# Column maxima of attention scores: subtraction on VectorE, or addition of the negated maxima by accumulating DMAs

## The chip, the cores and the metric

The kernel runs on one core of one Trainium2 chip. Its time is the device time of one execution in microseconds (us), lower is better; of several executions the median is taken. The core has five instruction queues: TensorE (PE; its weight loads are shown apart as PEld), VectorE (DVE), ScalarE (ACT), GpSimd (POOL) and SyncE (SP). All run side by side, each strictly in its own written order, and wait for each other by semaphores. SP computes nothing here: it issues DMAs, as POOL does too. The DMAs of both run on the same 16 DMA engines. Matrix products land in PSUM, everything else lives in SBUF or in HBM.

## What is computed

The reference takes a token matrix x (2048 tokens, width 448) and mixes two blocks by a sigmoid gate:

```
g = sigmoid((x * gate_w).sum(-1))
q, k, v = split heads of x @ wqkv          # 16 heads of width 28
a = softmax(q k^T * 28**-0.5) v @ wo       # full attention, 2048 x 2048 per head
b = (relu(x @ W_gate) * (x @ W_up)) @ W_down   # hidden width 1792
out = g * a + (1 - g) * b
```

All inputs and the output are float32. The softmax needs a maximum for each query row so that the exponent does not overflow.

## The kernel before

Keys stand on the partitions and queries along the free dimension: a *score* is a product of K (128 keys) with Q (512 queries), so the exponentials can go into the next product without a transpose. There are 16 heads; each is handled in two *visits* (one for each half of the 2048 keys), and each visit is one *round* of the main loop: 32 rounds, v = 0 to 31. Even rounds start a head, odd ones end it.

**Two ways to a maximum.** For three of the four blocks of 512 queries, `smax` multiplies Q with K once more (`sm`), takes the maximum along the free dimension on DVE (`mx`, line 171), and `smax_end` (`n` in the order strings) turns these row maxima by a small PE transpose (`mt`) and writes them over ACT (`mr`, `mh`), DVE and two DMAs (`Q<-mh`, line 188) into two extra rows of Q, where the score product subtracts them for nothing. This runs one to two heads ahead, and the first score of a new head has to wait for those two rows. For the fourth block of queries (j = 3, `TQ = 1`) the maximum is taken from the scores themselves: the scores are copied raw from PSUM to SBUF by ACT, `block_max` (line 228) folds them on DVE into `rm`, reading PSUM, `all_max` (`A`, line 234) takes the maximum over the partitions on POOL, `take_max` (`d`, line 239) subtracts `rm` from two quads of 128 x 2048 on DVE, and `take_exp` (`e`, line 246) exponentiates them on ACT. `rescale` (`c`, `f`) corrects the first visit's sums when the second visit found a larger maximum.

**The order of the work** is written out by hand. `FIRST`, `LONG`, `WIDE` and `LATE` are strings of one letter per piece of work, and `ROUNDS` says which string each round follows: round 0 is FIRST, the last three are LATE, four are WIDE and 24 are LONG. `s` is a score (two matmuls of 512 columns and the ACT copy or exp), `m` is an `smax` (two matmuls and a reduce), `x` is one matmul of the hidden layer (`gu`; 11 of them make a half unit, two halves a unit), `P` and `Q` are the two halves of the product with V (`po`), `w` prepares weights of the hidden layer (`split_f`: a high part by ACT, the rest `wg` on POOL, line 112). `score` runs `AHEAD` pieces into the next visit. PSUM gives scores and `sm` products three buffers of two banks in turn (`ps_w`), so each of them waits until the piece three places earlier has been read out. For the raw scores of block 3, that means read by ACT and by DVE.

**The DMA queue of SP** carries all loads in written order. `small_things(2v)` stands at a round's start and `small_things(2v + 1)` behind a certain `s`, the eighth. In an even round the first loads K and Q of the head after next (`load_k`, `load_q`: 8 DMAs of 28 rows of 8 KB), the second issues the row sums' reciprocals to HBM and their broadcast back (`l_d`, `rb`: `row_sums`, `spread`); SP waits in between until the first has landed. In the following odd round the first new `m` of the round reads the K and Q so loaded. The tokens X are replaced after each 14th unit (`gu_mm`), and the hidden layer's products go to HBM (`h_d`) until the attention is done. After round 31 the kernel runs the rest of the hidden layer, the output projection and the mix (`acc`, `wo`).

Of the kernel before, what the change touches and what calls it, by code (L numbers as in the profile page):

```python
# [9 lines left out]
F32 = mybir.dt.float32  # L10
# [9 lines left out]
P = 128  # L20
S = 2048
D = 448
H = 16
# [14 lines left out]

EARLY = (5, 4, 4, 3, 2, 2, 1, 1)

AHEAD = 3

NP = 10

FIRST = "AmxmxsmxmxxlxsxumsmmmxxxsxdxxxsxssmxxmxsmmxdexxsxsewsPQ"

LONG = "ssmnAxxxxsmxsxmxsmxxxmsmxxxsmxxmxsdxsxxxsxsmxxxsmxxmexxsmxxdxxcsxsefwsPQ"

WIDE = "smnmxxxxxxxsxxmxxxxmsxmxxsmxxsAmxsxmxxsxsmxdxsxxsssxxxmxxxcsxmsxxdxxmxxxxexsxewsPfQ"

LATE = "snwsxxAxdxxxsxxsxxxsxxdsxxxxcsxxsxxxsxxxsxxxxsxsxxxxsxxxxxexxxsxxessPfQ"
# [15 lines left out]
def gated_mix_kernel(ctx, tc, x, wq, wo, wgu, wd, out):  # L67
# [138 lines left out]

    stream = [p for v in range(2 * H) for p in visit(v)]
    todo_max, todo_sub, todo_exp, todo_all = [], [], [], []
    RM = {}

    def block_max(v, j, k, p, q):

        n = TQ[v // 2]
        b = j - NB + n
        if (v, b) not in RM:
            if b == 0:
                rm = att.tile([P, max(TQ), TB], F32, name=f"rm_{v}", tag=f"rm{v % 2}", bufs=1)
                for c in range(n):
                    RM[v, c] = rm[:, c]
        r = RM[v, b]  # L220
        if k % (NK // 2):
            parts = [(p[:, c], r) for c in range(2)]
        elif v % 2:
            parts = [(p[:, 0], RM[v - 1, b]), (p[:, 1], r)]
        else:
            parts = [(p[:, 0], q[:, 1])]
        for x, y in parts:
            nc.vector.tensor_tensor(r, x, y, op=OP.max)  # L228
        if k % (NK // 2) == NK // 2 - 2:
            todo_all.append((v, b, [(v, j, i) for i in (k // 4 - 1, k // 4)]))  # L230

    def all_max():
        v, b, quads = todo_all.pop(0)
        nc.gpsimd.partition_all_reduce(RM[v, b], RM[v, b], P, bass_isa.ReduceOp.max)  # L234
        todo_sub.extend((v, b, q) for q in quads)

    def take_max():
        v, b, q = todo_sub.pop(0)
        nc.vector.tensor_tensor(QUAD[q], QUAD[q], RM[v, b].unsqueeze(1).to_broadcast([P, 4, TB]), op=OP.subtract)  # L239
        todo_exp.append(q)  # L240

    def take_exp():
        q = min(todo_exp, key=lambda q: (q[0], q[2], q[1]))
        todo_exp.remove(q)
        q = QUAD[q].rearrange("p c t -> p (c t)")
        nc.scalar.activation(q, q, AF.Exp, scale=SCALE)  # L246

    def score(late=True):

        v, done, q, half, chunks = stream.pop(0)  # L250
        h = v // 2
        if q not in QUAD:
            QUAD[q] = p_slot(next(slots) % NP, f"P_{v}_{q[1]}_{q[2]}")
        ps = ps_w(f"s_{v}_{chunks[0][0]}_{chunks[0][1]}")
        for c, (k, j) in enumerate(chunks):
            nc.tensor.matmul(ps[:, c], K[h % 3][:, k * P:(k + 1) * P], Q[h][:, j * TB:(j + 1) * TB], start=True, stop=True)  # L256
            AT[v, k, j] = QUAD[q][:, 2 * half + c]
        dst = QUAD[q][:, 2 * half:2 * half + 2]
        if done:
            nc.scalar.activation(dst, ps, AF.Exp, scale=SCALE)  # L260
        else:
            nc.scalar.activation(dst, ps, AF.Copy)  # L262
            job = (v, chunks[0][1], chunks[0][0], ps if late else dst, dst)
            if late:
                block_max(*job)
            else:
                todo_max.append(job)

    X = {}

# [17 lines left out]
    with tc.tile_pool(name="qkv", bufs=1) as pa:  # L288
# [132 lines left out]

        warm = pa.tile([P, TB], BF16, name="warm")
        nc.vector.memset(warm, 0.0)
        ps = ps_x("warm_ps")
# [51 lines left out]
        for n, (f, *a) in enumerate(mixed):  # L476
            if n == 0:
                split_w(*w5)
            if n == 6:
                load_k(1)  # L480
                load_q(1)
            if n == 8:
                split_w(*w3)
            if n == 13:

                nc.gpsimd.memset(f32(K[2])[96:128], -1.0)
            if n == len(mixed) - 6:
# [8 lines left out]
            news = [(score, False) for back in EARLY if back == len(mixed) - n]  # L496
# [161 lines left out]
    split_f(0, act_high, pool_low, (0,))  # L658
    fetch_f(1)
    while todo_max:  # L660
        block_max(*todo_max.pop(0))
    for v, (order, nu) in enumerate(ROUNDS):
        todo = list(range(nxt, nxt + nu))
        nxt += nu
# [4 lines left out]
        for o in order:  # L669
            if o == "x" and not passes:  # L670
                continue
            if o == "s":
                ns += 1
                if ns == 8:
                    small_things(2 * v + 1)
                if stream:
                    score()
# [17 lines left out]
            elif o == "w":  # L695
                ready = nxt + (ROUNDS[v + 1][1] if v + 1 < len(ROUNDS) else 2)
                ready = min(ready + ready % 2, 2 * NF)
                while parts < ready:
                    split_f(parts // 2, act_high, pool_low, (parts % 2,))
                    parts += 1  # L700
                    if parts % 2 == 0:
                        fetch_f(parts // 2 + 1)
            elif o == "A":
                all_max()
            elif o == "d":
                take_max()
            elif o == "e":
                take_exp()
            elif o in "cf":
# [1 line left out]
            elif o == "l":  # L711
                sends.pop()()
            elif o == "u":
                split_f(0, act_high, pool_low, (1,))
# [8 lines left out]
        left = [k for k in todo_exp + todo_sub + todo_all if k[0] == v]  # L723
        assert not passes and not left and v not in PO or len(stream) == max(0, 16 * (2 * H - 1 - v) - AHEAD), (v, passes, left, len(stream) + 16 * (v + 1))
    assert not stream and m == len(maxima), (len(stream), m)
    stk.close()

# [181 lines left out]
```

## Time and profile before

| | us |
|---|---|
| median of 3 runs | 1289.12 (1284.76 to 1290.27) |
| the profiled execution | 1281.88, span 1280.1 |
| PE busy | 1241.6 (97%) |
| DVE busy | 962.1 (75%) |
| ACT busy | 776.1 (61%) |
| POOL busy | 191.2 (15%) |
| projections, up to the start of the main loop | 0 to about 136 |
| round 0 | about 136 to 177 |
| rounds 1 to 31 | 177 to 1080 |
| rest | 1080 to 1280 |

A row of the profile names engine, line and operation, then what is written and read (`rm<-s,rm`), its shape, how often it ran (x218), busy time and mean duration in ns, then the engine's idle time before it and who ended that. In the chain of waits, each row is a start, a duration and who held the chain: a stretch of DVE there is a time in which PE waited for DVE or worked on something that did not count. The PE matmuls are pipelined, so a row's duration (0.39 us for one) is longer than the spacing of two starts.

### The profile page before, as it was taken

How to read it: one execution, taken by the hardware profiler on the slowest of the kernel's cores; microseconds unless marked ns; L12 is line 12 of the kernel's file. 1: busy time of each engine (PE TensorE's matmuls, PEld its weight loads, DVE VectorE, ACT ScalarE, POOL GpSimd, SP SyncE). 2: the span in 40 equal slices, each digit the busy share in tenths (PEclk: the TensorE clock that was granted, in tenths of full speed). 3: DMA queues.
4: the chain of work that ended last, by engine and by line, in shares of the span. 5: the costliest groups of instructions: out<-in, count | busy, mean ns of one | idle time of the engine just before them, and what ended most of it. 6: DMA issues, size and time to landing. Idle time of an engine off the chain costs nothing.

```text
span 1280.1 us, 16867 instructions
## 1 busy us (share of the span) xinstructions
PE 1241.6 (97%) x6431; PEld 872.5 (68%) x6431; DVE 962.1 (75%) x1022; ACT 776.1 (61%) x894; POOL 191.2 (15%) x188
## 2 busy tenths in 40 slices
PE   9999699999999999999999999999999999999998
PEld 6888466665656666666666566666666566799998
DVE  6466679898988989998988889898989543563342
ACT  5223377777877677777777677767777784122121
POOL 4222221221221000000000001000000010551020
PEclk9999899999999999999999999999999999999999
DMA  9845275352626543342536243342442325745432
GB/s 323 289 189 222 84 209 117 127 163 72 169 76 201 169 121 84 103 133 64 163 104 186 81 113 103 84 130 93 132 128 76 119 90 195 228 147 159 132 115 80
DMA packets 64269, 178.37 MB, mean 139 GB/s; under 512 B 13730, under 2 KB 20578, under 8 KB 59554
## 3 DMA queue, kind: packets, MB, share of 16 engines
q1 hardware_dynamic: 57452, 151.00, 39.5%
q0 software_dynamic: 6304, 25.82, 5.3%
q8 instruction: 51, 0.84, 0.3%
q10 hardware_dynamic: 432, 0.46, 0.1%
q14 instruction: 30, 0.25, 0.1%
HBM read 118.58 MB, written 58.87 MB: 139 GB/s over the span
## 4 chain that ended last, share of the span: by engine, by line
PE 89%; DVE 4%; ACT 2%; DMA 2%; issue 1%; POOL 1%; SPq 0%; POOLq 0%; ACTq 0%
PE gu L547 19%; PE s L256 19%; PE po L601 18%; PE sm L169 13%; PE acc L808 10%; PE qk L381 5%; DVE rm L228 3%; PE wo L767 3%; PE v L399 3%; ACT P L262 1%; DVE mx L171 1%; DMA wg<-ws_d 1%; DMA or<-o_d 0%; DMA wr<-wq 0%; ACT P L260 0%
## 5 line engine op out<-in xcount | busy, mean ns | idle before, releaser
L171 DVE TENSOR_REDUCE mx<-sm 128x1 f32<-128x1024 f32 x384 | 456.5, 1219 | 60.6 <-PE sm L169 59.5
L547 PE MATMUL gu<-X,wg 128*128 128x512 f32 x1232 | 373.9, 398 | 10.8 <-POOL wg L112 7.2
L260 ACT ACTIVATE P<-s 128x1024 f32<-128x1024 f32 x306 | 306.7, 1025 | 116.8 <-PE s L256 113.1
L256 PE MATMUL s<-Q,K 128*128 128x512 f32 x1024 | 319.5, 403 | 13.6 <-DVE rm L228 11.2
L547 PEld LDWEIGHTS gu<-X,wg 128*128 128x128 f32 x1232 | 231.6, 189 | 69.1 <-POOL wg L112 7.6
L256 PEld LDWEIGHTS s<-Q,K 128*128 128x128 f32 x1024 | 184.7, 189 | 99.3 <-DVE rm L228 10.9
L169 PE MATMUL sm<-K,Q 128*128 128x512 f32 x768 | 243.2, 398 | 7.5 <-DVE mx L171 3.6
L601 PE MATMUL po<-P,V 128*32 128x512 f32 x1640 | 227.3, 594 | 0.0
L228 DVE TENSOR_TENSOR rm<-s,rm 128x512 f32<-128x512 f32 x218 | 150.4, 690 | 74.6 <-ACT P L262 57.3
L169 PEld LDWEIGHTS sm<-K,Q 128*128 128x128 f32 x768 | 137.1, 188 | 52.6 <-ACT P L260 10.1
L234 POOL PARTITION_ALL_REDUCE rm<-rm x32 | 57.2, 1788 | 673.7 <-DVE rm L228 618.8
L601 PEld LDWEIGHTS po<-P,V 128*32 128x32 f32 x1640 | 62.6, 110 | 116.2 <-issue 111.5
L808 PE MATMUL acc<-WD,hh 128*128 128x448 f32 x672 | 138.5, 365 | 0.0
L262 ACT ACTIVATE P<-s 128x1024 f32<-128x1024 f32 x104 | 105.1, 1024 | 46.6 <-PE s L256 45.4
L808 PEld LDWEIGHTS acc<-WD,hh 128*128 128x128 f32 x672 | 126.2, 188 | 10.4
L239 DVE TENSOR_TENSOR P<-P,rm 128x2048 f32<-128x2048 f32 x52 | 117.9, 2272 | 5.8 <-POOL rm L234 5.8
L601 PE MATMUL po<-V 128*32 128x512 f32 x408 | 115.0, 594 | 0.0
L103 ACT ACTIVATE hh<-hr 128x512 fp32r<-128x512 f32 x56 | 35.2, 631 | 117.8 <-PE acc L808 113.8
L246 ACT ACTIVATE P<-P 128x2048 f32<-128x2048 f32 x52 | 99.4, 1914 | 5.3 <-DVE P L239 4.5
L260 ACT ACTIVATE V<-s 128x1024 f32<-128x1024 f32 x78 | 78.9, 1025 | 37.1 <-PE s L256 35.2
L109 DVE TENSOR_TENSOR hh<-hr,hh 128x512 fp32r<-128x512 f32 x56 | 49.4, 883 | 62.2 <-ACT hh L103 62.2
L381 PE MATMUL qk<-X,W 128*128 128x512 f32 x308 | 77.4, 398 | 0.3 <-DVE X L109 0.2
(79 smaller groups left out, 772.4 us busy)
## 6 DMA issues: line engine op xcount, KB each, us to landing
wg<-ws_d SPq DMA_DIRECT2D x42, 896.0 KB
K<-qk_d SPq DMA_DIRECT2D x64, 224.0 KB
Q<-qk_d SPq DMA_DIRECT2D x64, 224.0 KB
h_d<-h SPq DMA_DIRECT2D x56, 256.0 KB
hr<-h_d SPq DMA_DIRECT2D x56, 256.0 KB
ws_d<-wg SPq DMA_DIRECT2D x14, 896.0 KB
qk_d<-st POOLq DMA_DIRECT2D x21, 512.0 KB, 3.2
wgr<-wgu SPq DMA_DIRECT2D x13, 512.0 KB
```

What stands on the lines that cost most here:

```text
L169: nc.tensor.matmul(ps[:, c, :], Q[h][:, u * P:(u + 1) * P], K[h % 3][:, k0:k0 + TB], start=True, stop=True)
L171: nc.vector.tensor_reduce(MX[h][:, 2 * u + half:2 * u + half + 1], ps, axis=AX.XY, op=OP.max)
L228: nc.vector.tensor_tensor(r, x, y, op=OP.max)
L239: nc.vector.tensor_tensor(QUAD[q], QUAD[q], RM[v, b].unsqueeze(1).to_broadcast([P, 4, TB]), op=OP.subtract)
L246: nc.scalar.activation(q, q, AF.Exp, scale=SCALE)
L256: nc.tensor.matmul(ps[:, c], K[h % 3][:, k * P:(k + 1) * P], Q[h][:, j * TB:(j + 1) * TB], start=True, stop=True)
L260: nc.scalar.activation(dst, ps, AF.Exp, scale=SCALE)
L262: nc.scalar.activation(dst, ps, AF.Copy)
L381: nc.tensor.matmul(ps, W[:, a, c * P:(c + 1) * P], xf(tb, b), start=(n == 0), stop=(n == NT - 1))
L547: nc.tensor.matmul(ps, WS[i][:, s, a], xf(i // NF, b), start=(n == 0), stop=(n == NT - 1))
L601: nc.tensor.matmul(po[32 * j:32 * j + 32], V[:, h // 4 % 2, k, h % 4], AT.pop((v, k, j)), start=(k == k0), stop=(k == k0 + NK // 2 - 1))
L808: nc.tensor.matmul(ACC[i // NF][t][:, :D], HH[i][:, a, t * P:(t + 1) * P], WD[:, f, b], start=(f == 0 and n == 0), stop=(f == NF - 1 and n ...
```

## The change

Seven things change together:

- **Maxima.** Scores of block 3 are copied with scale -1, so SBUF holds negated raw scores. `block_min` (`b`, three letters per visit) folds them on DVE from SBUF only: three operations of 128 x 1024, one of 128 x 512, and one that negates (and in odd visits takes the maximum with the first visit's). `rm` is the positive maximum as before.
- **Subtraction.** `take_max` now adds `rm` to the negated scores. With letter `d` this is a DMA from POOL that accumulates into SBUF (two of 1 MB per visit); with `g`, in round 0 alone, a DVE operation. The exponent's scale is negated.
- **POOL.** The hidden layer's weight rests (`low`) go from POOL to DVE, and a small all-reduce (`warm_r`) is run at the start of the program.
- **K and Q loads** go from the start of an even round to behind `row_sums` and `spread`, which now stand behind the tenth `s`.
- **Order strings.** All four are rewritten; `AHEAD` is 4, and `n` moves in LONG from the round's start to behind its ninth `s`.
- **WIDE rounds** are k = 2, 7, 10, 19, so that units 13, 27 and 41 end in a round's last `x`: the tokens are replaced there.
- **The extra Q buffer's** constant rows are copied by two DMAs, not set by POOL.

POOL in rounds 1 to 3 before. A bare `ISA` stands where POOL is configured for another kind of instruction; `rm` is the all-reduce, `wg` a weight rest:

```order
L234 ISA
L234 ISA rm_1_1302<-rm_1_1302 128x512
L112 ISA
L112 TENSOR_TENSOR wg_3_1567<-wgr_3_1326,wg_3_1567 128x384 x2
L112 TENSOR_TENSOR wg_3_1567<-wgr_3_1326,wg_3_1567 64x2x128
L234 ISA
L234 ISA rm_2_1553<-rm_2_1553 128x512
```

POOL in the same rounds now (P and V hold the quads):

```order
L238 ISA rm_1_0_1310<-rm_1_0_1310 128x512
L245 DMA P_1_3_2_1266<-rm_1_0_1310 128x4x512
L245 DMA P_1_3_3_1282<-rm_1_0_1310 128x4x512
L238 ISA rm_2_0_1553<-rm_2_0_1553 128x512
L245 DMA V_101<-rm_2_0_1553 128x4x512
L245 DMA P_2_3_1_1534<-rm_2_0_1553 128x4x512
```

The weight rests and the reconfigurations have gone from POOL, and each all-reduce is followed by its two accumulating DMAs.

SP in round 12 before (an even round; `ls` are the sums that the round before made):

```order
L611 DMA ls_5_4095<-os_5_3863 128x1x16
L148 DMA K2_104<-qk_d_71 28x2048 x4
L153 DMA Q2_1200<-Q2_1200 2x2048
L155 DMA Q2_1200<-qk_d_71 28x2048 x4
L566 DMA h_d_18_4174<-h_18_4172 128x512
L539 DMA wg_20_4176<-ws_d_6_2086 128x1792
L617 DMA l_d_5_85<-rq_5_4196 128x16
L623 DMA rb_5_4199<-l_d_5_85 32x512 x4
```

SP in round 12 now:

```order
L618 DMA ls_5_4104<-os_5_3855 128x1x16
L624 DMA l_d_5_85<-rq_5_4194 128x16
L630 DMA rb_5_4197<-l_d_5_85 32x512 x4
L148 DMA K2_104<-qk_d_71 28x2048 x4
L153 DMA Q2_1187<-Q2_1187 2x2048
L155 DMA Q2_1187<-qk_d_71 28x2048 x4
L573 DMA h_d_19_4245<-h_19_4243 128x512
L546 DMA wg_21_4247<-ws_d_7_2109 128x1792
```

The loads of K and Q have moved behind the wait of `rb` for `l_d`, and ahead of the round's last weight load.

PE at the start of round 13 before (a LONG round; `mt_7` is the transpose of head 7's row maxima, `s_14` are scores of that head):

```order
L256 MATMUL s_13_14_3_4340<-Q0_105,K0_102 128x512 x2
L256 MATMUL s_13_8_0_4346<-Q0_105,K0_102 128x512 x2
L169 MATMUL sm_192_4351<-K2_104,Q2_1200 128x512 x2
L181 MATMUL mt_7_4355<-ident_149,m_7_4264 16x128
L547 MATMUL gu_20_0_4365<-X0_111,wg_20_4176 128x512 x2
```

PE in round 13 now, from `mt_7` to the first score of head 7:

```order
L181 MATMUL mt_7_4436<-ident_151,m_7_4295 16x128
L554 MATMUL gu_21_0_4418<-X0_111,wg_21_4247 128x512
L264 MATMUL s_13_14_0_4447<-Q0_105,K0_102 128x512 x2
L169 MATMUL sm_198_4451<-K2_104,Q2_1187 128x512 x2
L554 MATMUL gu_21_0_4418<-X1_112,wg_21_4247 128x512
L264 MATMUL s_13_15_0_4456<-Q0_105,K0_102 128x512 x2
L554 MATMUL gu_21_0_4418<-X0_111,wg_21_4247 128x512 x2
L264 MATMUL s_13_14_2_4462<-Q0_105,K0_102 128x512 x2
L169 MATMUL sm_199_4466<-K2_104,Q2_1187 128x512 x2
L264 MATMUL s_14_0_3_4471<-Q1_106,K1_103 128x512 x2
```

Before, `s_14_0_3` stood 50 rows behind `mt_7`; now 14 matmuls stand between them.

The diff, cut to its core; of the order strings, one is shown:

```
-AHEAD = 3
+AHEAD = 4
-LONG = "ssmnAxxxxsmxsxmxsmxxxmsmxxxsmxxmxsdxsxxxsxsmxxxsmxxmexxsmxxdxxcsxsefwsPQ"
+LONG = "AssdmxxsxxmxscxdxsmsxxxmssxxxmsxmxnxsmxsxxsmsxxxsmsxbbxxsxebxxmfxxmxmxexwPQ"
-ROUNDS = [(FIRST, 2)] + [(WIDE, 4) if k % 7 == 2 else (LONG, 3) for k in range(2 * H - 4)] + [(LATE, 4)] * 3
+ROUNDS = [(FIRST, 2)] + [(WIDE, 4) if k in (2, 7, 10, 19) else (LONG, 3) for k in range(2 * H - 4)] + [(LATE, 4)] * 3
...
+    def block_min():
+
+        if not todo_max:
+            return
+        v, j, p = todo_max[0]
+        b = j - NB + TQ[v // 2]
+        if (v, b) not in R2:
+            R2[v, b] = att.tile([P, 2, TB], F32, name=f"r2_{v}_{b}", tag="r2", bufs=1)
+            left[v, b] = NK // 4 - 2
+            nc.vector.tensor_tensor(R2[v, b], todo_max.pop(0)[2], todo_max.pop(0)[2], op=OP.min)
+            return
+        nc.vector.tensor_tensor(R2[v, b], R2[v, b], todo_max.pop(0)[2], op=OP.min)
+        left[v, b] -= 1
+        if left[v, b]:
+            return
...
+        nc.vector.tensor_tensor(r, r2[:, 0], r2[:, 1], op=OP.min)
+        if v % 2:
+            nc.vector.scalar_tensor_tensor(r, r, -1.0, RM[v - 1, b], op0=OP.mult, op1=OP.max)
         else:
+            nc.vector.tensor_scalar(r, r, -1.0, None, op0=OP.mult)
...
-    def take_max():
+    def take_max(way):
         v, b, q = todo_sub.pop(0)
-        nc.vector.tensor_tensor(QUAD[q], QUAD[q], RM[v, b].unsqueeze(1).to_broadcast([P, 4, TB]), op=OP.subtract)
+        m = RM[v, b].unsqueeze(1).to_broadcast([P, 4, TB])
+        if way == "d":
+            nc.gpsimd.dma_start(QUAD[q], m, accum_op=OP.add)
+        else:
+            nc.vector.tensor_tensor(QUAD[q], QUAD[q], m, op=OP.add)
...
-            nc.scalar.activation(dst, ps, AF.Copy)
-            job = (v, chunks[0][1], chunks[0][0], ps if late else dst, dst)
...
+            nc.scalar.activation(dst, ps, AF.Copy, scale=-1.0)
+            todo_max.append((v, chunks[0][1], dst))
...
+        nc.gpsimd.partition_all_reduce(warm_r, warm_r, P, bass_isa.ReduceOp.max)
...
-        if q == 0 and h and h + 2 < H:
-            load_k(h + 2)
-            load_q(h + 2)
...
         if h and q == 1:
             row_sums(h - 1)
             spread(h - 1)
+            if h + 2 < H:
+                load_k(h + 2)
+                load_q(h + 2)
...
-                if ns == 8:
+                if ns == 10:
                     small_things(2 * v + 1)
...
-                    split_f(parts // 2, act_high, pool_low, (parts % 2,))
+                    split_f(parts // 2, act_high, low, (parts % 2,))
...
-                nc.gpsimd.memset(f32(QS[2])[96:128], 0.0)
+                for a, b in ((GD, 12), (GD + 12, 4)):
+                    nc.sync.dma_start(f32(QS[2])[a:a + b].rearrange("p j t -> p (j t)"), Q[1][GD + 2:GD + 2 + b].bitcast(F32))
```

More of the change, by code (lines that the diff above doesn't have):

```diff
@@ L208, in gated_mix_kernel @@
     todo_max, todo_sub, todo_exp, todo_all = [], [], [], []
[L209 to L224, printed above, removed]
-        else:
[L226 to L230, printed above, removed]
+    RM, R2, left = {}, {}, {}
+    def block_min():
[12 more added lines that the diff above has]
+            return
+        r, r2 = att.tile([P, TB], F32, name=f"rm_{v}_{b}", tag=f"rm{v % 2}{b}", bufs=1), R2[v, b]
+        RM[v, b] = r
+        nc.vector.tensor_tensor(r, r2[:, 0], r2[:, 1], op=OP.min)
+        if v % 2:
+            nc.vector.scalar_tensor_tensor(r, r, -1.0, RM[v - 1, b], op0=OP.mult, op1=OP.max)
+        else:
+            nc.vector.tensor_scalar(r, r, -1.0, None, op0=OP.mult)
+        q = NK // 8 * (v % 2)
+        todo_all.append((v, b, [(v, j, q), (v, j, q + 1)]))
     def all_max():
@@ L245, in take_exp, with score @@
         q = QUAD[q].rearrange("p c t -> p (c t)")
-        nc.scalar.activation(q, q, AF.Exp, scale=SCALE)
-    def score(late=True):
+        nc.scalar.activation(q, q, AF.Exp, scale=-SCALE)
+    def score():
         v, done, q, half, chunks = stream.pop(0)
@@ L423, in gated_mix_kernel @@
         nc.vector.memset(warm, 0.0)
+        warm_r = pa.tile([P, 16], F32, name="warm_r")
+        nc.vector.memset(warm_r, 0.0)
         ps = ps_x("warm_ps")
@@ L495, in gated_mix_kernel @@
                 m += 1
-            news = [(score, False) for back in EARLY if back == len(mixed) - n]
+            news = [(score,) for back in EARLY if back == len(mixed) - n]
             for k, c in enumerate(news):
@@ L722, in gated_mix_kernel @@
                 pv(v, "PQ".index(o))
-        left = [k for k in todo_exp + todo_sub + todo_all if k[0] == v]
-        assert not passes and not left and v not in PO or len(stream) == max(0, 16 * (2 * H - 1 - v) - AHEAD), (v, passes, left, len(stream) + 16 * (v + 1))
+        rest = [k for k in todo_exp + todo_sub + todo_all if k[0] == v]
+        assert not passes and not rest and v not in PO or len(stream) == max(0, 16 * (2 * H - 1 - v) - AHEAD), (v, passes, rest, len(stream) + 16 * (v + 1))
     assert not stream and m == len(maxima), (len(stream), m)
```

22 lines of the change are left out of this document (9 added, 13 removed).

## The prediction

> **What bounds the kernel now.** I read the engines' busy times first, then the chain that ended last, by engine:
>
> ```profile
> PE 1241.6 (97%) x6431; PEld 872.5 (68%) x6431; DVE 962.1 (75%) x1022; ACT 776.1 (61%) x894; POOL 191.2 (15%) x188
> PE 89%; DVE 4%; ACT 2%; DMA 2%; issue 1%; POOL 1%; SPq 0%; POOLq 0%; ACTq 0%
> ```
>
> PE is busy nearly always and holds 89% of the chain, so taking work off DVE is worth nothing by itself. Only the time in which PE is held up can be won. The stretches of round 0 (with the few microseconds ahead of it), of an odd LONG round (15) and of two even ones (16 and 20) show where that is; the columns are the stretch, its length, and the busy time of PE, PEld, DVE, ACT and POOL, then PE's clock, the DMA engines' share and GB/s:
>
> ```profile
> 136.00:177.50 41.50, 29.57 (x134) 17.49 (x133) 28.46 (x32) 19.93 (x27) 10.31 (x11) 0.84 0.43 116
> 588.80:617.70 28.90, 28.21 (x158) 18.34 (x155) 25.44 (x25) 22.02 (x24) 1.78 (x1) 1.00 0.17 58
> 617.70:646.70 29.00, 28.20 (x157) 18.21 (x153) 26.54 (x28) 19.97 (x19) 1.83 (x2) 1.00 0.67 184
> 735.70:764.50 28.80, 28.46 (x157) 18.24 (x153) 25.95 (x27) 20.40 (x20) 1.83 (x2) 1.00 0.46 122
> ```
>
> Round 0 leaves PE idle for 12 of 41.5 us, with its clock down to 0.84. In the others DVE is busy 25.4 to 26.5 of 29 us, close to full itself. The chain of waits through round 15 shows what that costs:
>
> ```profile
> 589.55 1.03 ACT P L262
> ...
> 590.61 0.70 DVE rm L228
> ...
> 591.34 0.70 DVE rm L228
> ...
> 592.17 0.70 PE s L256 x2
> ...
> 597.99 0.70 PE gu L547 x3
> ...
> 610.77 7.00 PE po L601 x64
> 617.77 0.43 PE s L256
> ```
>
> Three `gu` matmuls take 0.70 us, so 0.233 each. A LONG round has 16 `s` and 12 `m` of two matmuls and 33 `x`: 89 x 0.233 = 20.7 us, and 7.0 us of `po`: 27.7 us, against 28.9. So 1.2 us a round are lost, and nearly all of it at the start: `s` waits until ACT has copied the raw score and DVE has folded it twice from PSUM (`rm`). That is the ceiling of a round.
>
> **Round 0: -14 us.** The chain there, then POOL's rows:
>
> ```profile
> 135.68 0.70 DVE rm L228
> ...
> 141.43 1.15 DVE mx L171
> 142.61 1.07 PE sm L169 x2
> ...
> 149.45 6.58 issue
> 156.04 0.98 POOL wg L112
> 157.10 0.73 POOL wg L112
> 157.87 0.79 PE gu L547
> ```
>
> ```profile
> 144.31 1.80 POOL L234 PARTITION_ALL_REDUCE rm<-rm  x1 [5.62 <-DVE mx L171]
> 147.12 0.90 POOL L388 DMA_DIRECT2D qk_d<-pair  x1 [1.01 <-DVE pair L109]
> 156.04 1.78 POOL L112 TENSOR_TENSOR wg<-pair,wg 128x384 fp32r<-128x384 f32 x2 [8.01 <-issue]
> ...
> 186.88 1.80 POOL L234 PARTITION_ALL_REDUCE rm<-rm  x1 [6.83 <-DMA Q<-mh]
> ```
>
> Two things hold PE: a block of `rm` operations (135.7 to 141.4), and a weight rest that POOL starts 8.0 us after it was reconfigured from the all-reduce. The order shows that each such change of kind has a bare `ISA` row on POOL; now there is one at the start and one after round 31. The rest goes to DVE (row below: 0.50 us for 128 x 336), and the folds are spread over six `b`. Floor of the round by the same count: 24 pairs x 0.467 + 22 x 0.233 + 7.0 = 23.3 us, against 41.5. I leave 4 us for what stays in line (all-reduce 1.8 us and a DVE addition, 2.3 us as the subtraction's row below, ahead of the first exp): 27.3 us, so -14. Ends: -10, if the additions hold ACT and PE once more, and -17. The early `warm_r` puts its reconfiguration ahead of POOL's memsets and the first stores of `qk`; five staging buffers at 11 matmuls each cover some 13 us of that. I take 0; if the cover is short, up to +3.
>
> **Folding and subtracting: -17 us.** The groups of instructions (busy us, mean ns of one, idle time before):
>
> ```profile
> L171 DVE TENSOR_REDUCE mx<-sm 128x1 f32<-128x1024 f32 x384 | 456.5, 1219 | 60.6 <-PE sm L169 59.5
> ...
> L228 DVE TENSOR_TENSOR rm<-s,rm 128x512 f32<-128x512 f32 x218 | 150.4, 690 | 74.6 <-ACT P L262 57.3 <-ACT V L262 10.0 <-DVE rm L228 0.5
> ...
> L239 DVE TENSOR_TENSOR P<-P,rm 128x2048 f32<-128x2048 f32 x52 | 117.9, 2272 | 5.8 <-POOL rm L234 5.8
> ...
> L246 ACT ACTIVATE P<-P 128x2048 f32<-128x2048 f32 x52 | 99.4, 1914 | 5.3 <-DVE P L239 4.5
> ...
> L109 DVE TENSOR_TENSOR X<-xr,X 128x1024 fp32r<-128x1024 f32 x6 | 7.3, 1224 | 3.6 <-ACT X L103 3.5
> ...
> L109 DVE TENSOR_TENSOR W<-wr,W 128x336 fp32r<-128x336 f32 x6 | 2.8, 504 | 2.0 <-ACT W L103 1.9
> ```
>
> Per visit the folds were about 7 x 0.69 = 4.8 us and become 3 x 1.22 + 2 x 0.69 = 5.0 us: no gain in DVE's work. The gain is that they read SBUF, so a score's PSUM buffer is free after the 1.03 us copy. The two subtractions, 4.5 us a visit, leave DVE, which falls from some 26 to some 22 us a round; the weight rests add about 0.55 us each in rounds 0 to 8, inside that room. So the two `rm` waits at a round's start go. What is late next is ACT: 16 copies of 1.03 us and two exps of 1.9 us are in the way of the same PSUM buffers, and DVE now does its folds in a bunch ahead of the last `m`. I take half of the 1.2 us ceiling in each of 28 LONG and WIDE rounds: -17. Ends: 0 and -34.
>
> **The accumulating DMAs: 0.** Two of 1 MB a visit, 62 in all. No row shows one; the nearest is a plain 1 MB store from POOL, and the load that SP's queue puts on the DMA engines:
>
> ```profile
> x_d<-X POOLq DMA_DIRECT2D x6, 1024.0 KB, 5.1
> q1 hardware_dynamic: 57452, 151.00, 39.5%
> ```
>
> 5.1 us each from issue to landing, 10.2 us a pair, is the lower end; the upper is open. From the 16th score of a round to the first exp in the next there are 10.7 + 17.7 = 28.4 us of PE's written work (letters times the durations above); copy, fold, all-reduce and issue take 0.6 + 1.0 + 2.6 + 1.8 + 0.9 = 6.9 us of it. So the first quad has 21.5 us and both have 24 us. At 10.2 us they are hidden with room for twice that, and at 24 us a pair every further microsecond is paid in each round. I take the lower end's side, since engines loaded to 39.5% + 62 x 5.1 / 1280 = 64% still have room. The Trainium skill, in "Collectives: The Full Stack", section "The bandwidth ceiling: the fold count and why AG ≠ RS ≠ AR", has it that an add in the DMA path needs two source reads and runs at half a copy's rate; by that the pair would take 20.4 us, still inside the 24, but with the engines at 89%.
>
> **K and Q loads: +2 us.** Round 20 and the start of 21 before:
>
> ```profile
> 737.24 2.37 SPq L148 DMA_DIRECT2D K<-qk_d  x4
> ...
> 749.02 0.35 SPq L617 DMA_DIRECT2D l_d<-rq  x1
> 750.48 1.69 SPq L623 DMA_DIRECT2D rb<-l_d  x4
> ...
> 767.74 1.95 SPq L188 DMA_DIRECT2D Q<-mh  x2
> ```
>
> ```profile
> 746.00:747.00 1.00, 1.00 (x6) 0.79 (x6) 0.83 (x2) 0.98 (x1) 0.00 (x0) 1.00 0.96 205
> 747.00:748.00 1.00, 1.00 (x6) 0.82 (x5) 1.00 (x2) 0.05 (x1) 0.00 (x0) 1.00 0.38 82
> ```
>
> The loads keep the DMA engines full from 738 to 747.5, 10.3 us after the first issue. Now the first K load is issued behind `rb`: `l_d` at 12.1 us into the round (13.3 here; the reciprocal now stands behind the sixth reduce, not the eighth), 1.5 us to land, 1.7 us for `rb`: 15.3 us. Done at 25.6. The first `m` of the new head stands 0.9 us into the next round, at about 28.9. Room: 3.3 us, which the next visit's accumulating DMAs, issued from about 24 us on, eat into. Queued behind the wait on SP are the round's last `h_d` and weight load, needed a unit later. I take 2 us over 13 loads; ends 0 and +13 (1 us each).
>
> **Row maxima of the next head: +6 us.** Before, `mt` at 766.03, and the chain behind it:
>
> ```profile
> 766.03 0.27 PE L181 MATMUL mt<-ident,m 128*16 128x128 f32 x1
> 768.82 0.30 DVE L109 TENSOR_TENSOR mh<-mr,mh 16x128 fp32r<-16x128 f32 x1
> ```
>
> The second `Q<-mh` leaves SP at 769.69, and a small DMA lands in 1.5 us less its issue of 0.35: 4.8 us after `mt`. Then a score 50 rows later waited for it; now 14 matmuls lie between, 14 x 0.233 + 0.27 = 3.5 us. So PE would wait up to 1.3 us in each of the 12 odd LONG rounds, +15. But 1.2 us of the 4.8 are DVE finishing two `rm` and a reduce first, which are gone; I take +0.5 us each. Lower end 0.
>
> **The rest.** Token reloads at a round's end: `gu` waits for them in no row above 1 us, 0. AHEAD, Q's constant rows: 0, covered by PE's own work.
>
> **Sum.** -14 - 17 + 2 + 6 = -23. The profiled execution took 1281.88 us, which gives 1259; the median of the runs shown is 7.2 us above it, and against that the forecast is 1289 - 23 = 1266 us.
>
> **Rivals.**
> - *Slower: the accumulating DMAs crowd out the exps.* They share 16 engines with K, Q, weights and `h_d`. The point from which it decides is a pair taking 24 us from issue to landing. At 27 us, three microseconds in 28 rounds are +84: 1289 - 23 + 84 = 1350. For it: K and Q loads alone keep the engines at up to 0.96 for 10 us of every second round. Against it: over the whole of odd round 15 they stand at 0.17. The Trainium skill's "DMA: Bandwidth & Descriptors", section "Issuing engines are not separate DMA queues", says that POOL's and SP's DMAs run on the same engines and interleave, which would delay both.
> - *About the same: the waits are only exchanged.* Row maxima +15, K and Q loads +13, the rest as forecast: 1289 - 31 + 28 = 1286. For it: room of 3.3 us and a shortage of 1.3 us are both small against what I cannot see.
> - *The whole ceiling:* -17 in round 0 and -34 in the rounds, no new wait: 1238. For it: PE waits for nothing else in these rounds.
> - *It does not do what it says:* PE waits on ACT's copies alone, and only round 0 is won: 1289 - 14 = 1275; inside the forecast's own range.
>
> **Chances.** Forecast 0.50, with a range of its own from 1250 to 1279; ceiling 0.12; exchanged waits 0.16; slower 0.22. From no change, 0.5% is 6.4 us, about what can be told apart here. Exchanged waits lie, with their own spread, mostly within that and in part on the faster side: faster 0.50 + 0.12 + 0.06 = 0.68, same 0.10, slower 0.22. The range runs from 1244 (half of the ceiling) to 1300 (the exchanged waits and the mild end of slower); some 0.05 lie below and 0.15 above.
>
> **What would show it.** Round 0 at 26 to 29 us with PE's clock at 1.00; LONG rounds at 28.2 to 28.6 us; no wait of PE `s` for DVE `rm`; DVE near 840 us busy (962 - 62 x 2.27 + 28 x 0.55 + 32 x 0.2); accumulating DMAs landing within 5 to 11 us; POOL with no idle of 6 to 8 us behind a change of kind before the tail. Wrong would be: ACT waiting for a DMA ahead of the exp, PE `sm` waiting for K or Q at the start of odd rounds by more than 0.2 us, PE `s` waiting for `Q<-mh` by more than 1 us.

## Result and profile after

The changed kernel takes 1353.35 us (median, 1352.82 to 1354.58) against 1287.33 us of the kernel before beside it: ratio 1.051, 95% interval 1.0485 to 1.0541. It is 5% slower; the forecast was 1266 us, in a range of 1244 to 1300. (The scores are what is negated: the DMAs add the maxima as they are.)

The page of the changed kernel, in the order of the prediction's fences: busy times, the chain by engine and by line, the two DMA queues with data, and the accumulating DMAs (count, KB each, median us from issue to landing):

```profile
PE 1259.5 (93%) x6431; PEld 881.2 (65%) x6431; DVE 851.4 (63%) x923; ACT 773.3 (57%) x894; POOL 232.0 (17%) x208
PE 68%; DMA 21%; DVE 4%; SPq 2%; ACT 2%; issue 1%; POOL 0%; DVEq 0%; POOLq 0%
...
q1 hardware_dynamic: 57484, 151.13, 36.8%
q0 software_dynamic: 39040, 90.84, 32.3%
...
P<-rm POOLq DMA_DIRECT2D x50, 1024.0 KB, 12.7
V<-rm POOLq DMA_DIRECT2D x12, 1024.0 KB, 13.8
```

DVE is down by 111 us, about as forecast, and PE is held up all the same: its share falls from 97% to 93%, and DMAs, 2% of the chain before, are 21% now. POOL's queue (q0) has gone from 5.3% to 32.3% of the DMA engines' time. Its line before:

```profile
q0 software_dynamic: 6304, 25.82, 5.3%
```

The waits of PE in the changed kernel, and one of DVE (us in all, how often, longest):

```profile
PE s L264 <- DMA Q<-mh: 41.3, 13, 8.6
PE sm L169 <- DVE mx L171: 15.1, 8, 5.2
PE gu L554 <- DMA X<-x_d: 11.3, 6, 4.7
...
DVE rq L623 <- DMA ls<-os: 27.7, 9, 9.5
```

None of these waits is for the accumulating DMAs. Their consumer, the exp, does not wait at all (the last number is ACT's idle time before it):

```profile
L254 ACT ACTIVATE P<-P 128x2048 f32<-128x2048 f32 x52 | 98.4, 1912 | 0.3
```

Three stretches show the gain and the loss side by side: round 0, the even LONG round 10, and the odd LONG round 15 (stretch, length, busy time of PE, PEld, DVE, ACT and POOL, PE's clock, DMA share, GB/s):

```profile
137.00:168.60 31.60, 24.68 (x133) 13.95 (x132) 30.21 (x32) 20.32 (x27) 4.51 (x5) 1.00 0.55 150
485.43:513.39 27.96, 27.96 (x161) 17.96 (x153) 22.18 (x23) 19.53 (x19) 4.36 (x3) 1.00 0.87 191
633.25:667.66 34.41, 30.71 (x161) 19.94 (x154) 22.09 (x22) 21.98 (x23) 4.58 (x5) 0.90 0.56 137
```

Round 10 has no idle PE left: 27.96 us against 28.9 before, the whole ceiling of 1.2 us within 0.3 us. Round 15 holds the same matmuls and takes 6.45 us more.

**How round 15 loses them.** SP's queue (issues), then the chain of waits, then PE's row of that score (in brackets the idle time before it and who ended it):

```profile
643.51 0.38 SPq L546 DMA_DIRECT2D wg<-ws_d  x1
645.31 1.18 SPq L188 DMA_DIRECT2D Q<-mh  x2
```

```profile
645.95 5.50 DMA Q<-mh
...
651.59 1.19 PE s L264 x2
```

```profile
651.59 1.19 PE L264 MATMUL s<-Q,K 128*128 128x512 f32 x2 [3.70 <-DMA Q<-mh]
```

SP issues a weight load of 896 KB and, 1.8 us behind it, the two small DMAs that carry the row maxima of the next head. These take 5.5 us to land, and the first score of that head waits 3.7 us. The wait costs more than itself, as the clock shows (third number from the end):

```profile
640.00:647.40 7.40, 7.40 (x34) 5.77 (x33) 6.40 (x7) 6.40 (x9) 0.00 (x0) 1.00 1.10 234
647.40:651.60 4.20, 0.50 (x4) 0.09 (x2) 1.22 (x1) 1.08 (x2) 0.00 (x0) 0.82 0.44 176
651.60:656.00 4.40, 4.40 (x11) 3.43 (x12) 0.19 (x1) 2.64 (x3) 0.00 (x0) 0.50 0.00 0
656.00:660.00 4.00, 4.00 (x17) 3.23 (x16) 3.79 (x4) 3.00 (x3) 0.00 (x0) 0.88 0.02 4
```

The DMA engines are full before the wait (in the DMA share, the last number but one, more than 1 means that the packets' times add up to more than the stretch). Counted by queue in the trace, 0.95 of that 1.10 are POOL's queue, the accumulating DMAs: the pair issued at 630.7 moves its packets from 633.2 to 648.5, and half of the weight load's packets of 7 KB, issued at 643.5, start only after 648.0. So `Q<-mh` stands behind a load that the accumulating DMAs hold up. The clock is at 0.50 from 650.2 to 656.9 and at 1.00 again from 657 (0.88 is the mean of a stretch that holds both). PE works 5.3 us of this at half speed, which costs 2.7 us; with the 3.7 us of the wait that is 6.4 of the 6.45 us lost.

**How even rounds lose.** Round 6, SP's issues (the first and the last of four transfers for the hidden layer's weights, `ws_d` and `wgr` in turn, and the row sums) and the chain:

```profile
343.79 0.54 SPq L539 DMA_DIRECT2D ws_d<-wg  x1
...
347.17 1.30 SPq L289 DMA_DIRECT2D wgr<-wgu  x1
348.57 1.17 SPq L618 DMA_DIRECT2D ls<-os  x1
```

```profile
348.57 12.62 DMA ls<-os
...
361.21 0.25 DVE rq L623
361.47 1.09 DVE mx L171
...
362.60 1.22 PE sm L169 x2
```

The row sums `ls`, 8 KB, are queued behind these four, of 512 or 896 KB each, and land after 12.6 us. The accumulating pair issued at 339.6 has its packets on the engines from 341.5 to 358.5, beside them. DVE's reciprocal `rq` waits for them, every later reduce waits behind `rq`, and PE waits 5.2 us for a PSUM buffer that such a reduce still has to read.

### The profile page after: what moved, and what is told of

Same layout as the page of the kernel before. It is cut to its first block, busy times and chain, and to the rows that moved or that the text cites. A ratio compares the mean times of both kernels' runs of the same rounds, so it can differ in the third digit from the quotient of the medians.

```text
span 1351.0 us, 16885 instructions
## 1 busy us (share of the span) xinstructions
PE 1259.5 (93%) x6431; PEld 881.2 (65%) x6431; DVE 851.4 (63%) x923; ACT 773.3 (57%) x894; POOL 232.0 (17%) x208
## 3 DMA queue, kind: packets, MB, share of 16 engines
q1 hardware_dynamic: 57484, 151.13, 36.8%
q0 software_dynamic: 39040, 90.84, 32.3%
## 4 chain that ended last, share of the span: by engine, by line
PE 68%; DMA 21%; DVE 4%; SPq 2%; ACT 2%; issue 1%; POOL 0%; DVEq 0%; POOLq 0%
PE gu L554 14%; PE po L608 14%; PE s L264 12%; PE acc L816 10%; PE sm L169 9%; DMA ls<-os 7%; PE qk L385 5%; DMA Q<-mh 5%; PE wo L775 3%; PE v L403 2%; DMA X<-x_d 2%; DVE mx L171 2%; DMA wgr<-wgu 2%; DMA wg<-ws_d 1%; DMA Q<-qk_d 1%
## 5 line engine op out<-in xcount | busy, mean ns | idle before, releaser
L171 DVE TENSOR_REDUCE mx<-sm 128x1 f32<-128x1024 f32 x384 | 463.1, 1221 | 225.4 <-PE sm L169 222.8
L554 PE MATMUL gu<-X,wg 128*128 128x512 f32 x1232 | 384.5, 406 | 17.4 <-DMA X<-x_d 11.3
L264 PE MATMUL s<-Q,K 128*128 128x512 f32 x1024 | 328.5, 412 | 47.2 <-DMA Q<-mh 41.3
L268 ACT ACTIVATE P<-s 128x1024 f32<-128x1024 f32 x306 | 301.7, 1028 | 115.9 <-PE s L264 109.3
L554 PEld LDWEIGHTS gu<-X,wg 128*128 128x128 f32 x1232 | 237.8, 193 | 81.3 <-DMA X<-x_d 10.8
L264 PEld LDWEIGHTS s<-Q,K 128*128 128x128 f32 x1024 | 188.3, 194 | 132.2 <-issue 54.4
L169 PE MATMUL sm<-K,Q 128*128 128x512 f32 x768 | 245.6, 403 | 20.4 <-DVE mx L171 15.1
L169 PEld LDWEIGHTS sm<-K,Q 128*128 128x128 f32 x768 | 140.1, 192 | 67.0 <-DVE mx L171 19.8
L270 ACT ACTIVATE P<-s 128x1024 f32<-128x1024 f32 x104 | 104.5, 1034 | 61.0 <-PE s L264 58.1
L567 DVE TENSOR_TENSOR h<-gu,rl 128x512 f32<-128x512 f32 x56 | 38.5, 688 | 71.4 <-ACT rl L564 24.0
L385 PE MATMUL qk<-X,W 128*128 128x512 f32 x308 | 77.9, 398 | 0.4 <-DVE X L109 0.2
L245 POOL DMA_DIRECT2D P<-rm x50 | 68.8, 1579 | 8.6 <-POOL rm L238 8.6
## 6 DMA issues: line engine op xcount, KB each, us to landing
P<-rm POOLq DMA_DIRECT2D x50, 1024.0 KB, 12.7
V<-rm POOLq DMA_DIRECT2D x12, 1024.0 KB, 13.8
```

The lines of the kernel that those rows point to most:

```text
L169: nc.tensor.matmul(ps[:, c, :], Q[h][:, u * P:(u + 1) * P], K[h % 3][:, k0:k0 + TB], start=True, stop=True)
L171: nc.vector.tensor_reduce(MX[h][:, 2 * u + half:2 * u + half + 1], ps, axis=AX.XY, op=OP.max)
L245: nc.gpsimd.dma_start(QUAD[q], m, accum_op=OP.add)
L270: nc.scalar.activation(dst, ps, AF.Copy, scale=-1.0)
L385: nc.tensor.matmul(ps, W[:, a, c * P:(c + 1) * P], xf(tb, b), start=(n == 0), stop=(n == NT - 1))
L554: nc.tensor.matmul(ps, WS[i][:, s, a], xf(i // NF, b), start=(n == 0), stop=(n == NT - 1))
```

## Experiments

Two theories stood at first. A: the row maxima are too late by their place in the order, and each wait lowers the clock behind it. B: the accumulating DMAs crowd the 16 DMA engines, and everything that is loaded comes late. Each ratio below is to the kernel before on the same chip, with its 95% interval.

### The row maxima earlier

```
-LONG = "AssdmxxsxxmxscxdxsmsxxxmssxxxmsxmxnxsmxsxxsmsxxxsmsxbbxxsxebxxmfxxmxmxexwPQ"
+LONG = "AssdmnxxsxxmxscxdxsmsxxxmssxxxmsxmxxsmxsxxsmsxxxsmsxbbxxsxebxxmfxxmxmxexwPQ"
```

> The changed kernel, with the letter n of LONG (the transpose of the next head's row maxima) moved from 14 matmuls ahead of the head's first score back to the start of the round. Theory A (scores wait for the row maxima, whose small DMAs are queued behind a weight load, and the clock falls behind each such wait; in the changed kernel these waits are 41 us, and the idle of PE lowers its clock): the wait of scores for Q<-mh falls from 41 us to under 2 us, the odd LONG rounds 5, 7, 13, 17 and 19 from 31.6-36.0 us to 28-30 us, the whole to 1285-1305 us. Theory B (the accumulating DMAs crowd the 16 DMA engines, so that everything which is loaded comes late): the waits move to other loads, and the time stays at 1335 us or above.

Measured: 1329.25 us, 1.033 (1.031 to 1.036). The same round 15, and round 9:

```profile
627.98:656.02 28.04, 28.04 (x161) 18.10 (x154) 22.19 (x22) 21.26 (x23) 4.60 (x5) 1.00 0.63 153
441.66:483.61 41.95, 32.52 (x161) 19.37 (x154) 21.41 (x21) 22.17 (x24) 4.51 (x4) 0.88 0.70 194
```

Round 15 is cured, and so are 13 and 19 (28.0 us each); the whole falls by 24 us only. Round 9 is lost to another load: PE waits there four times, 8.4 us in all, for the tokens X that are replaced at the end of round 8. The wait for `Q<-mh` stays at 23.8 us, in rounds 1, 3, 5, 7, 23, 25, 27 and 29. A explains a third of the 66 us and no more.

### The addition on DVE in all rounds

```
-                take_max(o)
+                take_max("g")
```

> The changed kernel, with all additions of the maxima made by DVE and no accumulating DMA. Theory A: the waits for Q<-mh stay at 20 us or more, since the row maxima are still late; the waits for the row sums ls<-os and for the tokens X shrink; DVE rises to about 960 us; 1310-1340 us. Theory B: the waits for DMAs go altogether, 1260-1285 us.

Measured: 1342.11 us, 1.043 (1.041 to 1.045). Neither theory has it. PE's waits:

```profile
PE s L264 <- DVE mx L171: 33.9, 34, 2.8
PE po L608 <- ACT P L254: 10.1, 5, 2.8
PE s L264 <- DMA Q<-mh: 4.8, 4, 2.1
```

The waits for DMAs are nearly gone, `Q<-mh` too, though `n` stands where it stood: this points to the accumulating DMAs as what made the row maxima late, though rounds that are slower for another reason give the row maxima more time too. The order is laid out for DMAs: an addition of 2.3 us on DVE now stands between reduces that PE needs, and in WIDE and LATE rounds the second one stands so near the round's end that `po` waits for the exp behind it. This run says which waits go with the DMAs, not what they cost.

### The row maxima's DMAs in ACT's queue

```
-            nc.sync.dma_start(f32(Q[h])[GD + r:GD + r + 1], f32(mh)[:, r])
+            nc.scalar.dma_start(f32(Q[h])[GD + r:GD + r + 1], f32(mh)[:, r])
```

> The changed kernel, with the two small DMAs of each set of row maxima issued from ACT's queue in place of SP's; all else, the place of n too, as it is. Theory A, in the form that the two small DMAs wait behind the weight load in the same queue: they land within 3.5 us of the transpose in all rounds, the wait for them falls from 41 us to under 8 us, 1290-1315 us. Theory B (the 16 engines themselves are crowded, whatever the queue): they land as late as before, 1340 us or above.

Measured: 1345.1 us, 1.046 (1.044 to 1.048).

```profile
PE s L264 <- DMA Q<-mh: 14.9, 7, 3.8
...
PE s L264 <- ACT P L268: 9.9, 10, 1.8
```

Away from the weight load the wait falls by 26 us, so a large part of it was the place in SP's queue; the time is as theory B had it all the same. The wait of scores for ACT's copies is new (9.9 us, 0.4 in the changed kernel); that it comes from ACT issuing the two DMAs in its own order is likely but not shown. And the waits that are left still bring the clock down: round 15 takes 33.9 us with two of 0.6 and 1.9 us. Only 8 us are won.

### The WIDE rounds where they were

```
-ROUNDS = [(FIRST, 2)] + [(WIDE, 4) if k in (2, 7, 10, 19) else (LONG, 3) for k in range(2 * H - 4)] + [(LATE, 4)] * 3
+ROUNDS = [(FIRST, 2)] + [(WIDE, 4) if k % 7 == 2 else (LONG, 3) for k in range(2 * H - 4)] + [(LATE, 4)] * 3
```

> The changed kernel, with the WIDE rounds where they stood before (k = 2, 9, 16, 23), so that tokens are replaced in the middle of a round. Theory A: the 22 us for which gu waits for X in rounds 9 and 27 shrink or move, the waits for Q<-mh stay; 1330-1350 us. Theory B: the same within 1335-1355 us, since the accumulating DMAs then meet the token loads elsewhere.

Measured: 1350.33 us, 1.052 (1.049 to 1.055). The wait for X falls from 11.3 to 8.0 us (the 22 us of the expectation count PE's weight loads beside its matmuls), and the ratio is no lower than the changed kernel's 1.051: where tokens are replaced matters little.

So the theories were put anew. C: the accumulating DMAs load the engines so much that SP's loads, and what is queued behind them, come late. D: the places of `n` and of the K and Q loads do it, whatever else runs.

### No addition at all

```
-        if way == "d":
-            nc.gpsimd.dma_start(QUAD[q], m, accum_op=OP.add)
-        else:
+        if way == "g":
             nc.vector.tensor_tensor(QUAD[q], QUAD[q], m, op=OP.add)
```

> The changed kernel with the addition of the maxima left out in rounds 1 to 31 (neither DMA nor DVE does it; the exponentials of block 3 are taken of the raw scores there, so this part of the output is not the reference's). Theory C (the accumulating DMAs load the DMA engines so much that SP's loads, and the small transfers queued behind them, come late): the waits for Q<-mh, ls<-os and X, 41, 28 and 22 us now, fall under 10 us together, LONG rounds 27.9-28.6 us, the whole 1245-1275 us. Theory D (the places of n and of the K and Q loads make the row maxima and the loads late, whatever else runs): Q<-mh still holds scores for 15 us or more, 1295 us or above.

This kernel leaves the addition out in rounds 1 to 31, so its output is wrong there. Measured: 1264.82 us, 0.984 (0.982 to 0.986). Two of PE's waits, and the busy times:

```profile
PE s L262 <- DMA Q<-mh: 6.4, 6, 2.3
...
PE gu L552 <- DMA X<-x_d: 1.1, 1, 1.1
...
PE 1234.4 (98%) x6431; PEld 865.6 (69%) x6431; DVE 849.4 (67%) x923; ACT 769.4 (61%) x894; POOL 150.3 (12%) x146
```

This decides it for C; `rq` too waits for `ls` once, 1.9 us, not nine times. The rest of the change is worth about 20 us, and the accumulating DMAs cost 1353.35 - 1264.82 = 88.5 us (about 86 if the 2.7 us by which the kernel before beside the two differs are taken off). By stretches of the trace (a round ends with its last `po` matmul), in us:

| | before | after | no addition |
|---|---|---|---|
| up to the end of round 0 | 177.0 | 168.6 | 168.7 |
| rounds 1 to 9 | 263.8 | 316.9 | 261.1 |
| rounds 10 to 28 | 557.8 | 578.3 | 547.4 |
| rounds 29 to 31 | 74.5 | 77.9 | 74.5 |
| the rest | 207.0 | 209.4 | 210.0 |

Most of the cost, 56 us, lies in rounds 1 to 9, where SP also carries the weights that are split for the hidden layer (`ws_d`, `wgr`). PE's waits of the two runs differ by 65 us (`Q<-mh` 34.9, reduces 15.1, X 10.2, and 5 us of small ones). The remaining 24 us are the clock, 0.974 against 0.997 over the span: for the same 6431 matmuls PE is busy 25 us longer with the accumulating DMAs (1259.5 against 1234.4 us).

### Plain DMAs in their place

```
-            nc.gpsimd.dma_start(QUAD[q], m, accum_op=OP.add)
+            nc.gpsimd.dma_start(QUAD[q], m)
```

> The changed kernel with plain DMAs in place of the accumulating ones: as many, as large, from the same queue at the same places, but they overwrite the scores with the maxima (this part of the output is not the reference's). Theory C, with the addition as what costs: packets of 2 KB take 84-98 ns against 176-190 ns, the DMAs land in 6-9 us against 12.7, and the waits shrink by half or more: 1275-1315 us. If the number and the bytes alone did it, the time stays at 1340 us or above. Theory D: 1300-1330 us, with the waits for Q<-mh at 20 us or more.

These DMAs overwrite the scores, so this output is wrong too. Measured: 1281.63 us, 0.998 (0.996 to 0.999). The queue with data and the DMAs of this run:

```profile
q0 software_dynamic: 23168, 90.84, 18.6%
...
P<-rm POOLq DMA_DIRECT2D x50, 1024.0 KB, 7.6
```

As many bytes cost 17 us instead of 88. Without them the queue took 5.4% of 1261.6 us, so a plain DMA of 1 MB costs (0.186 x 1278.5 - 0.054 x 1261.6) / 62 = 2.7 us of all 16 engines, and an accumulating one (0.323 x 1351.0 - 68.1) / 62 = 5.9 us. It goes in (39040 - 6304) / 62 = 528 packets, the plain one in 272: nearly all are of 2 KB in the first and of 4 KB in the second, and in the traces they take 184 and about 172 ns on average, so a byte costs about twice as much.

### K and Q loads back at the round's start

```
+        if q == 0 and h and h + 2 < H:
+            load_k(h + 2)
+            load_q(h + 2)
...
-            if h + 2 < H:
-                load_k(h + 2)
-                load_q(h + 2)
```

> The changed kernel with the loads of K and Q back at the start of even rounds, ahead of the row sums. Theory C: they then meet the second half of the previous visit's accumulating DMAs, the row sums come later, the time stays within 1340-1375 us. Theory D: 1325 us or below, since the row sums' chain and the maxima no longer have those loads around them late in the round.

Measured: 1404.23 us, 1.093 (1.091 to 1.096), worse than either theory expected.

```profile
PE sm L169 <- DVE mx L171: 47.1, 15, 7.4
...
DVE os L634 <- DMA rb<-l_d: 63.4, 8, 11.0
...
DVE rq L623 <- DMA ls<-os: 44.5, 14, 9.5
```

With the additions by DMA, 1.75 MB ahead of the row sums delays DVE in 14 rounds, not 9. The move of these loads is a gain of about 51 us under this load.

### One addition by DMA, the other on DVE

On top of the first experiment:

```
-        for o in order:
+        for i_o, o in enumerate(order):
...
-                take_max(o)
+                take_max("g" if order[:i_o].count("d") else o)
```

> The changed kernel with n of LONG back at the round's start (1329 us by itself), and only the first of each visit's two additions as an accumulating DMA, the second on DVE. Theory C: the DMA load of the additions halves, the waits for DMAs fall from 38 us to under 15 us, DVE rises to about 910 us: 1285-1310 us. Theory D: no change to speak of against 1329 us, 1318-1335 us.

Measured: 1325.3 us, 1.030 (1.028 to 1.033). The wait for `Q<-mh` is gone and X is at 5.0 us, but scores wait 28.2 us for reduces and `po` 14 us for the exp: the second addition stands in the wrong place for DVE, as before. So the places were chosen next: DVE is idle for 2.2 us during `po`, right before a round's first `m`. WIDE and LATE got their `A` and additions at the start too.

```
-LONG = "AssdmnxxsxxmxscxdxsmsxxxmssxxxmsxmxxsmxsxxsmsxxxsmsxbbxxsxebxxmfxxmxmxexwPQ"
+LONG = "AgssdmnxxsxxmxscxxsmsxxxmssxxxmsxmxxsmxsxxsmsxxxsmsxbbxxsxebxxmfxxmxmxexwPQ"
```

> The changed kernel with n of LONG at the round's start, the first addition of each visit on DVE at the very start of the round (behind the all-reduce, where DVE has 2.2 us of idle time while PE makes the po product), and the second an accumulating DMA a few letters later, in all strings. Theory C (the DMA engines' load is what costs, and it falls with the number of accumulating DMAs): half the load costs at most a third of the 88 us that both cost, as long as DVE's part does not stand in front of reduces: 1270-1292 us. If half the load costs half, 1300-1315 us.

Measured: 1284.72 us, 0.998 (0.997 to 1.000), as good as no change and as theory C had it. With `n` at the round's start in both, half of the accumulating DMAs at good places costs 45 us less than all of them (1329.25 us).

### Additions on POOL

The same strings with the second addition (`p`), and then both, as POOL instructions:

```
-            nc.vector.tensor_tensor(QUAD[q], QUAD[q], m, op=OP.add)
+            (nc.vector if way == "g" else nc.gpsimd).tensor_tensor(QUAD[q], QUAD[q], m, op=OP.add)
```

> The same with the second addition on POOL as an instruction, no DMA at all. POOL adds 128 x 384 in 0.96 us, so 128 x 2048 in about 5.1 us, with 6-8 us of reconfiguration before it and as much before the next all-reduce: some 21 of 28 us of a round. Theory C: 1262-1278 us, and no wait for a DMA above 3 us outside the tail. If POOL's and DVE's operations hold each other up, DVE's reduces take longer than 1.22 us and it is 1285 us or above.

> The same with both additions on POOL: 6-8 us, 2 x 5.1 us, 6-8 us and the all-reduce of 1.8 us, 24-28 us of a round's 28. Theory C: if it fits, 1262-1275 us; if POOL is the bound, rounds of 29-32 us and 1290-1340 us, with ACT's exp waiting for POOL.

Measured: 1331.57 us, 1.036 (1.034 to 1.038), and 1315.36 us, 1.025 (1.020 to 1.029). Both are above what theory C had. But POOL is not the bound: no exp waits for it, and even LONG rounds take 27.9 us in the second. Most odd ones lose 3 to 9 us, and PE's waits are for reduces, 49 us in all. DVE's rows there, one of round 3 and two of round 23, and POOL's of round 23:

```profile
235.81 4.34 DVE L109 TENSOR_TENSOR mh<-mr,mh 16x128 fp32r<-16x128 f32 x1
...
856.41 1.22 DVE L171 TENSOR_REDUCE mx<-sm 128x1 f32<-128x1024 f32 x1 [0.34 <-PE sm L169]
857.67 4.36 DVE L592 TENSOR_TENSOR rs<-rm,rm 32x512 f32<-32x512 f32 x1
```

```profile
856.90 4.57 POOL L247 TENSOR_TENSOR P<-P,rm 128x2048 f32<-128x2048 f32 x1 [7.64 <-issue]
861.45 4.99 POOL L247 TENSOR_TENSOR V<-V,rm 128x2048 f32<-128x2048 f32 x1
```

The reduce, which reads PSUM, runs beside POOL's addition in its usual 1.22 us. `rs`, which reads two operands from SBUF and takes 0.69 us alone, takes 4.36, and `mh`, 0.28 us alone, takes 4.34 in round 3 (a WIDE one). `rs` ends 0.6 us after POOL's addition, as if it had begun only then. The Trainium skill, "SBUF — State Buffer", section "SBUF: two separate sides", has this rule: a DVE operation with two SBUF inputs and a GpSimd operation that reads SBUF share one pair of ports, and the later one is blocked until the other ends. The trace agrees. So the operations of that kind were moved out of the way:

```
-LONG = "ApsspmnxxsxxmxscxxsmsxxxmssxxxmsxmxxsmxsxxsmsxxxsmsxbbxxsxebxxmfxxmxmxexwPQ"
+LONG = "nApsspmxxsxxmxsxxsmsxxxmssxxxmsxmxxsmxsxxsmscxxxsmsxbbxxsxebxxmfxxmxmxexwPQ"
```

> Both additions on POOL as in the run before, and the two small DVE operations that lay beside them there and took 4.2-4.4 us (mh, 0.28 us alone, and rs, 0.69 us alone) moved out of their way: n to the very start of LONG and WIDE rounds, c of LONG some 10 us later. Theory C with the two engines holding each other up as the reason of the run before: the odd LONG rounds fall from 31-37 us to 28-29 us, reduces are late nowhere, 1250-1272 us. If the additions on POOL slow PE or the reduces in another way, the odd rounds stay above 30 us and it is 1290 us or above.

Measured: 1255.76 us, 0.977 (0.975 to 0.978): 2.3% faster than before and 97.6 us faster than the changed kernel. An even and an odd LONG round (22 and 23), and POOL in the odd one:

```profile
774.64:802.60 27.96, 27.96 (x161) 17.96 (x153) 22.09 (x23) 19.56 (x19) 11.04 (x4) 1.00 0.47 119
802.60:830.77 28.17, 28.17 (x162) 17.91 (x154) 21.52 (x22) 21.74 (x24) 11.01 (x3) 1.00 0.29 94
```

```profile
807.53 4.63 POOL L247 TENSOR_TENSOR P<-P,rm 128x2048 f32<-128x2048 f32 x1 [7.66 <-issue]
812.13 4.60 POOL L247 TENSOR_TENSOR V<-V,rm 128x2048 f32<-128x2048 f32 x1
826.36 1.81 POOL L238 PARTITION_ALL_REDUCE rm<-rm  x1 [9.63 <-DVE rm L232]
```

PE has no idle time in either, and no wait of PE for `Q<-mh` shows among those of 0.9 us and more. POOL, idle for most of the time in both kernels, carries 9.2 us of additions and its reconfigurations in a round of 28 us. That this run is 9 us below the one without additions goes for the most part with the place of `n`: rounds 13, 15, 17 and 19, where scores waited for the row maxima there, took 29.5 to 30.6 us there and take 28.2 to 28.7 here.

## Why the prediction was wrong

**The step that failed: the accumulating DMAs at 0.** I measured the room of the one who waits for them, the exp, and that room was there: the exp waits 0.3 us in all. I took neither a loss from the others on the same 16 engines into the sum, nor looked at who that would be. Without these DMAs the kernel takes 1264.8 us, within 1.2 us of the forecast; with them 88.5 us more. Against the kernel before beside it the run without them won 20 us where -23 was forecast, and that is in part luck: round 0 won 6 us less than forecast, the other rounds 4 us more, and the rest of the kernel took 3 us longer. The load itself was close (64% forecast, 36.8 + 32.3 = 69% measured; the forecast took 5.1 us of all engines for a megabyte, measured 5.9, and left out the 5.3% that POOL's queue had before), so a mean share was the wrong measure: what matters is that an 8 KB transfer stands behind a megabyte in the rounds where the engines are full.

**Landing in 5 to 11 us:** wrong, 12.7 and 13.8 us. By the rule of the Trainium skill ("Collectives: The Full Stack", half rate for an add, which the page states for ReduceScatter) the estimate is 5.1 x 2 = 10.2 us each; measured is 5.9 / 2.7 = 2.2 times the engine time of a plain DMA, so the trace agrees with the rule. Its sum, 20.4 us a pair and hidden, was as wrong as mine, for the same reason.

**The rival "crowd out the exps", 1350 us**, came out at the measured time by another way, which is luck: of the 50 accumulating DMAs into P the median took 12.7 us to land and only the longest 24.2, and the exps waited 0.3 us in all. Crowded out were `Q<-mh`, `ls` and X, all on SP's queue. The Trainium skill's rule that the queues' DMAs run on the same engines and interleave ("DMA: Bandwidth & Descriptors", "Issuing engines are not separate DMA queues") agrees with the trace in part: POOL's DMAs held up SP's, and the row maxima sent from ACT's queue still made PE wait 14.9 us; but 26 us of that wait did go with the queue. The other rivals: the whole ceiling was won in the undisturbed rounds alone, waits were more than exchanged, and the change did what it says.

**Round 0, -14:** -8.4 measured. POOL's 8 us wait is gone, as forecast. The floor was too low, since I counted PE's work: in the 31.6 us DVE is busy 30.2, so DVE is the bound there. The weight rests, moved to it, were not in the sum of the round, and the additions, which DVE made there before as subtractions, only as 2.3 us in line.

**Folding and subtracting, -17; K and Q loads, +2; row maxima, +6 (together -9):** with no addition, rounds 1 to 28 take 808.5 us against 821.6, so -13. Undisturbed rounds won 0.95 us, not the half of 1.2 that I took; the wait for `Q<-mh` was 6.4 us, as forecast; no wait for K or Q showed. Under the accumulating DMAs two of these come out otherwise: the row maxima's later place costs 24 us (1353.35 against 1329.25), four times the forecast, and the later K and Q loads gain about 51 us where a loss of 2 was forecast.

**Tokens, 0:** 1.1 us of waits with no addition, 11.3 with them.

**What would show it:** DVE near 840 (851), no PE wait for `rm`, no reconfiguration in POOL's way: right. LONG rounds of 28.2 to 28.6: the undisturbed ones are faster, the others up to 43 us. Of the signs of a wrong forecast, PE waiting for `Q<-mh` by over 1 us was the one that came.

## What to carry to other kernels

Before moving work to DMAs, list every small transfer on a chain that PE waits for, whatever queue issues it, and see which large transfers will be ahead of it in each round; the room of the new DMA's own consumer says nothing on that. When such an operation only moves off a busy engine, look at the idle engine first: POOL did it here without holding PE up, once DVE's operations with two SBUF inputs stood clear of it. A change with several parts is best priced with the suspected work left out, which here split +66 us into about -20 and +86 in one run.

## What was not expected of the hardware

- An accumulating DMA within SBUF took 2.2 times the engine time of a plain one of the same bytes (5.9 against 2.7 us per MB over 16 engines).
- A wait of 3.7 us cost PE 6.45 us, since its clock stood at 0.50 from 650.2 to 656.9, 5.3 us of it behind the wait; in the run with ACT's queue, waits of 0.6 and 1.9 us left round 15 5.9 us longer (33.90 against 27.96): its clock stood at 0.50 from 645.1 to 651.9, and at 0.90 in the mean of the round:

```profile
645.71 1.19 PE L264 MATMUL s<-Q,K 128*128 128x512 f32 x2 [1.88 <-DMA Q<-mh]
...
628.28:662.18 33.90, 31.39 (x161) 20.18 (x154) 22.09 (x22) 21.87 (x23) 4.58 (x5) 0.90 0.56 131
```

- A DVE operation of 0.28 us (`mh`, 16 x 128) took 4.3 us beside POOL's addition, and a reduce from PSUM no longer than alone.
